# Heads of a linear attention in partition halves, zero rows written by count, and fewer weights split ahead

## The chip, the cores and the metric

The kernel runs on one core of a Trainium2 chip. The metric is the device time of one execution in microseconds (us). Engines: PE is TensorE (matmuls and transposes), DVE is VectorE, ACT is ScalarE, POOL is GpSimd, and SP issues most of the transfers.

## The reference, cut to what matters

Three stages on 3072 tokens (4 batches of 768), model width 384 (8 heads of 48).

```python
# 1: linear attention with a decaying state, per batch b and head h
for t in range(S):
    y[t]  = r[t] @ (state + outer(u * k[t], v[t]))
    state = w[:, None] * state + outer(k[t], v[t])
# 2: each token goes to one of 8 experts (384 -> 1024 -> 384, relu)
e_idx = argmax(x @ w_gate)
out[mask] = gate_w * sigmoid(x @ w_output_gate)[e] * (relu(x[mask] @ w1[e]) @ w2[e])
# 3: a dense layer pair, 384 -> 2048 -> 384
h = x @ w_in;  y = (h * cos(h)) @ w_out
```

## The kernel before, in words

The order of instructions on every engine is that of the program text; nothing is rescheduled.

**Attention** (`attention`). The 24 units are chunks of 128 tokens, unit i being chunk i // 4 of batch i % 4. With the decay powers `pw` and their inverses `ip`, a chunk becomes matrix products: `tr` transposes k (scaled to `kc` by POOL in `kprep`) and r, two heads (96 partitions) at a time. ACT copies the transposed k twice, each time with the mask `jm` that zeroes the other head, so that the score product of a head (L307, 96 rows) meets zeros in the rows of its neighbour. DVE scales the transposed r (L298) and masks the scores (L309). `state` multiplies r with the running state Z of the batch (L319, a 96x96 block per pair of heads; `blk` in `wd` keeps its off-diagonal blocks zero) and updates Z by L325, L327 and L328. `outp` adds scores times v (L341, output rows in two halves of 64) and DVE adds the bonus term (L343). Then `xt`, `logits` and, per batch of up to four units, `route1`, `prefix` and `route2` find the expert of each token and its row in the DRAM buffer `xd`, to which POOL scatters the token (L114). POOL also makes `rk` (L270, L273) and `dv` (L279), which waits for the row sums `dd` of DVE (L277).

In loop round i the text has: loads of unit i + 3, POOL's preparation of unit i + 2, `tr(i + 1)`, `scores(i)`, `xt(i - 1)`, `state(i)`, `logits(i - 1)`, routing, `dsum(i + 1)`, `outp(i)`, `prefix`. In rounds 1 to 4 SP writes zeros over the first 416 rows of each of the 8 regions of `xd`. In rounds 5 to 13 the first five pairs of expert weights are loaded, and from round 8 on they are split (`split_w`: ACT rounds to fp32r, DVE takes the remainder).

**Experts** (`moe`). After the attention come two branches that are not taken here (`any_decay` at L593, `overflow` at L695), which all engines pass. Then 64 steps, 8 blocks of 128 hidden columns for each expert. Step s loads and splits weights ahead (raw tiles in a ring of three, split tiles in a ring of seven), runs `l1` of its own block, `low` (DVE, the remainder of relu) of step s - 1 and `l2` of step s - 2. The rows of the next expert are loaded at block 0. **Dense layers** (`mlp2`) follow; they are not touched.

Of the kernel before, what the change touches and what calls it, by code (L numbers as in the profile page):

```python
# [28 lines left out]
NP = H // 2  # L29
NU = B * NCH  # L30
# [5 lines left out]
REG = N + OV  # L36
# [8 lines left out]
PRE = 5  # L45
# [18 lines left out]
class Program:  # L64
    def __init__(self, ctx, tc, r, k, v, w, u, w_gate, w_og, w1, w2, w_in, w_out, out):
# [10 lines left out]
        self.xd = dram.tile([E * REG, ROW], F32, name="xd")  # L76
        self.xg = dram.tile([S, B * DM], F32, name="xg")
# [119 lines left out]
    def attention(self, ctx):  # L197
# [9 lines left out]

        def load(i):
            c, b = divmod(i, B)
            for src, dst, nm in ((self.k, kt, "kt"), (self.r, rt, "rt"), (self.v, vt, "vt")):  # L210
                t = p2.tile([C, H, D], F32, tag=nm, name=nm, bufs=4 if nm == "vt" else 3)
# [3 lines left out]
        wT = ps.tile([96, NP], F32, tag="sm", name="wTp")  # L215
        nc.tensor.transpose(wT, self.wrow, ident[:NP, :NP])
# [9 lines left out]
        jm = cp.tile([96, 2], F32, name="jm")  # L226
        blk = cp.tile([96, 96], F32, name="blk")
        nc.gpsimd.memset(blk, 0.0)
        nc.gpsimd.affine_select(out=blk, in_=blk, compare_op=ALU.is_gt, fill=1.0, base=1 - D, pattern=[[-D, 2], [0, D]], channel_multiplier=1)
        nc.gpsimd.affine_select(out=blk, in_=blk, compare_op=ALU.is_ge, fill=0.0, base=0, pattern=[[-D, 2], [0, D]], channel_multiplier=1)  # L230
        nc.gpsimd.tensor_copy(jm, blk[:, ::D])

        pw = cp.tile([96, NP, C + 1], F32, name="pw")
        ip = cp.tile([96, NP, C], F32, name="ip")
# [3 lines left out]
        wTp, wT = wT, cp.tile([96, NP], F32, name="wT")  # L238
        nc.scalar.copy(wT, wTp)

        def double(t, o, n, eng):
            eng.tensor_tensor(t[:, :, o + n:o + 2 * n], t[:, :, o:o + n], t[:, :, o + n - 1:o + n].to_broadcast([96, NP, n]), ALU.mult)
# [18 lines left out]
        pwk = cp.tile([C, NP, 96], F32, name="pwk")  # L261
# [19 lines left out]
        def tr(i):  # L281
            s = st.setdefault(i, {})
            kT = ps.tile([96, NP, C], F32, tag="kT", name="kT")
            s["kT"] = p2.tile([96, NP, 2, C], F32, name="kTs")
            kk = s["kc"] if i else kt[i].rearrange("p (a j) d -> p a (j d)", j=2)
# [4 lines left out]
            rT = ps.tile([96, NP, C], F32, tag="rT", name="rT")  # L290
            rr = rt[i].rearrange("p (a j) d -> p a (j d)", j=2)
            for p in range(NP):
                nc.tensor.transpose(rT[:, p, :], rr[:, p, :], ident)
            s["rT"] = p2.tile([96, NP, C], F32, name="rTs")
            for p in ((slice(0, NP),) if i else (slice(0, 2), slice(2, 4))):
                if i == 0:
                    nc.vector.tensor_tensor(s["kT"][:, p], s["kT"][:, p], bc(ip[:, p], 2, 2), ALU.mult)
                nc.vector.tensor_tensor(s["rT"][:, p], rT[:, p], pw[:, p, 0:C], ALU.mult)  # L298

        def scores(i):  # L300
            s = st[i]
            s["A"] = []
            for q in range(2):
                A = ps.tile([C, 4, C], F32, tag=f"A{q}", name="A")
                for j in range(4):
                    h = 4 * q + j
                    nc.tensor.matmul(A[:, j, :], s["kT"][:, h // 2, h % 2, :], s["rT"][:, h // 2, :], start=True, stop=True)  # L307
                As = p2.tile([C, 4, C], F32, tag=f"As{q}", name="As")
                nc.vector.tensor_tensor(As, A, bc(amask, 1, 4), ALU.mult)  # L309
                s["A"].append(As)  # L310

        def state(i):
            s = st[i]
            c, b = divmod(i, B)
            if c:
                y = ps.tile([C, NP, 96], F32, tag="y", name="y")
                s["y"] = y
# [4 lines left out]
            P = ps.tile([96, NP, 96], F32, tag="P", name="P")  # L322
            vv = vt[i].rearrange("p (a j) d -> p a (j d)", j=2)
            for p in range(NP):
                nc.tensor.matmul(P[:, p, :], s["kc"][:, p, :], vv[:, p, :], start=True, stop=True)  # L325
            if c:
                nc.vector.tensor_tensor(Z[b], P, Z[b], ALU.add)  # L327
                nc.vector.tensor_tensor(Z[b], Z[b], wd, ALU.mult)  # L328
            else:
                Z[b] = cp.tile([96, NP, 96], F32, name=f"Z{b}")  # L330
                nc.vector.tensor_tensor(Z[b], P, wd, ALU.mult)

        def outp(i):
            s = st[i]
            c, b = divmod(i, B)
            y = s["y"] if c else ps.tile([C, NP, 96], F32, tag="y", name="y")
            for h in range(H):
                p, j = divmod(h, 2)
                for q in range(2):
                    t = slice(q * 64, q * 64 + 64)  # L340
                    nc.tensor.matmul(y[t, p, j * D:(j + 1) * D], s["A"][h // 4][:, h % 4, t], vt[i][:, h, :], start=(c == 0 and h == 0), stop=(h == H - 1))  # L341
            x = new_x(i)
            nc.vector.tensor_tensor(x[:, 0:DM], y.rearrange("p a d -> p (a d)"), s["dv"].rearrange("p h d -> p (h d)"), ALU.add)  # L343
# [16 lines left out]
        def logits(i):  # L360
# [3 lines left out]
            lg = ps.tile([128, 2 * E], F32, tag="sm", name="lg")  # L364
# [25 lines left out]
        def prefix(k):  # L390
            j, n = batches[k]
            for b in range(n):
                nc.vector.tensor_tensor(self.pf[:, j + b + 1, :], self.pf[:, j + b, :], self.ohall[:, j + b, :], ALU.add)

        def route2(k):
# [3 lines left out]
            rk = ps.tile([128, B, E], F32, tag="sm" if k < K - 1 else "xT", name="rkp")[:, 0:n]  # L399
# [39 lines left out]
        def totals():  # L439
            cnt = ps.tile([128, E], F32, tag="sm", name="cntp")  # L440
# [17 lines left out]
        def any_decay():  # L458
            st_ = p2.tile([96, 2, B * NP, D], F32, tag="kTs", name="gen_s")
            vs_ = p2.tile([96, 2, B * NP, D], F32, tag="As0", name="gen_v")  # L460
# [3 lines left out]
            uT = cp.tile([96, NP], F32, name="uT")  # L464
            nc.sync.dma_start(uT, self.u.rearrange("(p j) d -> (j d) p", j=2))
            nc.vector.memset(state_, 0.0)
# [40 lines left out]
        for p in range(NP):  # L507
            nc.tensor.transpose(tp[:, p * 96:(p + 1) * 96], ip[:, p, :], ident[:96, :96])
        nc.scalar.copy(pwk.rearrange("p a d -> p (a d)"), tp[:, :DM])
# [9 lines left out]
        wd = cp.tile([96, NP, 96], F32, name="wd")  # L519
# [350 lines left out]
```

## Time and profile before

| | us |
|---|---|
| median of 3 runs | 832.38 |
| lowest and highest | 830.17, 834.43 |
| the profiled execution, its own time | 830.15 |
| its span | 828.2 |
| PE busy in the span | 790.0 |
| DVE busy | 563.5 |
| ACT busy | 390.6 |
| POOL busy | 208.4 |

The attention fills the first 176 us or so, the experts run from about 186 to 410 us, the dense layers from there to the end. A matmul of f32 operands shows as two records. The idle time behind a group is that of its engine just before it, with what ended it.

### The profile page before, as it was taken

The numbers are of one execution on the slowest core, as the hardware profiler recorded it, in microseconds if no ns is written. First come the engines' busy times: TensorE is split into PE (matmuls) and PEld (weight loads), VectorE is DVE, ScalarE is ACT, GpSimd is POOL, SyncE is SP. The second block draws the span as 40 slices with busy tenths as digits, with TensorE's granted clock in tenths as the row PEclk, the third lists the DMA queues.
The fourth block names the chain that finished last, engine by engine and source line by source line (L and its number), as shares of the span: only waits on it lengthen the run. The fifth ranks groups of instructions, "written<-read, shape, count | busy, mean of one in ns | idle before, by whom it ended". The sixth has DMA issues, their size and how long they took to land.

```text
span 828.2 us, 14233 instructions
## 1 busy us (share of the span) xinstructions
PE 790.0 (95%) x5329; PEld 739.3 (89%) x5329; DVE 563.5 (68%) x987; ACT 390.6 (47%) x680; POOL 208.4 (25%) x290
## 2 busy tenths in 40 slices
PE   7989999929999999999999999999999999999996
PEld 7988899829999999999979999999999999988885
DVE  7778999736767777677376767767675555655653
ACT  3334343314555455545275655546464544445442
POOL 7667777620000000000021111111111122331332
PEclk9999999968999999999999999999999999999998
DMA  9897765136656654664201202102100201211211
GB/s 175 234 209 175 157 128 124 68 86 166 185 155 182 183 161 131 182 175 134 39 1 38 77 1 77 43 36 76 40 39 1 76 20 59 77 39 38 77 69 47
DMA packets 131304, 82.38 MB, mean 99 GB/s; under 512 B 83483, under 2 KB 123771, under 8 KB 131219
## 3 DMA queue, kind: packets, MB, share of 16 engines
q1 hardware_dynamic: 127717, 71.64, 32.5%
q0 software_dynamic: 3072, 9.45, 3.1%
q8 instruction: 45, 0.74, 0.4%
q14 instruction: 41, 0.33, 0.1%
q10 hardware_dynamic: 429, 0.21, 0.1%
HBM read 61.98 MB, written 19.31 MB: 98 GB/s over the span
## 4 chain that ended last, share of the span: by engine, by line
PE 72%; issue 2%; POOL 1%; DVE 1%; ACT 1%; POOLq 0%; ACTq 0%
PE h L756 8%; PE o L800 7%; PE h L757 7%; PE o L798 7%; PE o L799 7%; PE h L755 7%; PE h L627 4%; PE h L625 4%; PE acc L645 4%; PE h L626 4%; PE acc L647 4%; PE acc L646 4%; PE trp L608 1%; POOL out L114 1%; POOL nn L765 0%
## 5 line engine op out<-in xcount | busy, mean ns | idle before, releaser
L765 POOL TENSOR_SCALAR nn<-tt 128x512 f32<-128x512 f32 x96 | 60.1, 626 | 545.5 <-ACT tt L763 533.4
L766 DVE SCALAR_TENSOR_TENSOR tt<-nn,tt 128x512 f32<-128x512 f32 x96 | 66.4, 692 | 120.1 <-POOL nn L765 120.1
L763 ACT ACTIVATE tt<-h,quart 128x512 f32<-128x512 f32 x96 | 65.9, 686 | 77.4 <-PE h L757 76.9
L779 ACT CAST ga<-tt 128x512 fp32r<-128x512 f32 x96 | 59.7, 622 | 74.4 <-PE o L799 66.9
L159 DVE TENSOR_TENSOR wring<-raw,wring 128x768 fp32r<-128x768 f32 (+1 forms) x69 | 61.9, 897 | 45.9 <-ACT wring L158 45.9
L780 DVE TENSOR_TENSOR gc<-tt,ga 128x512 fp32r<-128x512 f32 x96 | 66.9, 697 | 17.7 <-ACT ga L779 17.6
L158 ACT CAST wring<-raw 128x768 fp32r<-128x768 f32 (+1 forms) x69 | 54.4, 788 | 44.1 <-PE acc L647 37.3
L800 PE MATMUL o<-wfix,gc 128*128 128x384 f32 x216 | 72.9, 338 | 0.1
L798 PE MATMUL o<-wfix,ga 128*128 128x384 f32 x216 | 72.7, 337 | 0.0
L799 PE MATMUL o<-wfix,ga 128*128 128x384 f32 x216 | 72.5, 336 | 0.0
L645 PE MATMUL acc<-hh,wring 128*128 128x416 f32 x192 | 69.0, 359 | 0.0
L771 ACT ACTIVATE tt<-tt 128x512 f32<-128x512 f32 x96 | 60.5, 630 | 17.7 <-DVE tt L766 17.7
L627 PE MATMUL h<-xs,wring 128*128 128x416 f32 x192 | 68.0, 354 | 0.0
L625 PE MATMUL h<-xs,wring 128*128 128x416 f32 x192 | 68.0, 354 | 0.0
L626 PE MATMUL h<-xs,wring 128*128 128x416 f32 x192 | 67.8, 353 | 0.0
L647 PE MATMUL acc<-hh,wring 128*128 128x416 f32 x192 | 67.1, 349 | 0.0
L646 PE MATMUL acc<-hl,wring 128*128 128x416 f32 x192 | 67.1, 349 | 0.0
L772 DVE TENSOR_TENSOR tt<-h,tt 128x512 f32<-128x512 f32 x96 | 65.7, 685 | 1.3 <-ACT tt L771 0.7
L756 PE MATMUL h<-ys,wfix 128*128 128x512 f32 x162 | 64.0, 395 | 0.2 <-DVE ys L747 0.2
L755 PE MATMUL h<-ys,wfix 128*128 128x512 f32 x162 | 63.1, 390 | 1.1 <-ACT ys L746 1.1
L757 PE MATMUL h<-ys,wfix 128*128 128x512 f32 x162 | 64.1, 395 | 0.0
L629 ACT ACTIVATE hh<-h 128x416 fp32r<-128x416 f32 x64 | 33.1, 517 | 52.8 <-PE h L627 49.9
(170 smaller groups left out, 1919.6 us busy)
## 6 DMA issues: line engine op xcount, KB each, us to landing
raw<-in_moe_w SPq DMA_DIRECT2D x128, 192.0 KB
raw<-in_moe_w_in SPq DMA_DIRECT2D x16, 384.0 KB
raw<-in_moe_w_out SPq DMA_DIRECT2D x16, 384.0 KB
xd<-rows SPq DMA_DIRECT2D x8, 625.6 KB
kt<-in_k SPq DMA_DIRECT2D x24, 192.0 KB
rt<-in_r SPq DMA_DIRECT2D x24, 192.0 KB
vt<-in_v SPq DMA_DIRECT2D x24, 192.0 KB
part<-osb SPq DMA_DIRECT2D x6, 768.0 KB
```

The costliest lines, as they stand in the source:

```text
L625: nc.tensor.matmul(h, wh, xh[:, kk, :], start=(kk == 0), stop=False)
L626: nc.tensor.matmul(h, wh, xl[:, kk, :], start=False, stop=False)
L627: nc.tensor.matmul(h, wl, xh[:, kk, :], start=False, stop=(kk == KD - 1))
L645: nc.tensor.matmul(acc[e][d], wh, a, start=(fb == 0), stop=False)
L646: nc.tensor.matmul(acc[e][d], wh, b, start=False, stop=False)
L647: nc.tensor.matmul(acc[e][d], wl, a, start=False, stop=(fb == NF1 - 1))
L755: nc.tensor.matmul(h, wh, xh[:, kk, :], start=(kk == 0), stop=False)
L756: nc.tensor.matmul(h, wh, xl[:, kk, :], start=False, stop=False)
L757: nc.tensor.matmul(h, wl, xh[:, kk, :], start=False, stop=(kk == KD - 1))
L798: nc.tensor.matmul(acc[k][q], a[:, sl], wh, start=(g == first), stop=False)
L799: nc.tensor.matmul(acc[k][q], a[:, sl], wl, start=False, stop=False)
L800: nc.tensor.matmul(acc[k][q], c[:, sl], wh, start=False, stop=(g == end))
```

## The change

Heads lie in halves of the partitions: each head has 64 rows, 48 used and 16 zero, so a pair of heads fills 128. The score and state products take 48 rows from partition 0 or 64, the state is 128x192 instead of 96x384, and the masked copies of k are gone; the k and r tiles are padded to 64 columns. The tile `y` takes two PSUM banks, and logits and ranks share the bank of `xT`. The copy of token ids goes to POOL, as do the prefix passes of all batches but the last three. Only region 0 of `xd` and a block of zeros in DRAM (`zd`) are written during the attention; for experts 1 to 7, `clear_rows` writes 416 zero rows behind the tokens of a region, from DRAM to DRAM, at an address from the count. Three weight pairs are loaded during the attention and none is split there: two are split after `totals`, and the expert loop catches up.

```diff
-REG = N + OV
+REG = N + CAP
-PRE = 5
+PRE = 2
+NRAW = 3
+        self.zd = dram.tile([CAP, ROW], F32, name="zd")
...
-        self.wrow = cp.tile([NP, 96], F32, name="wrow")
-        nc.sync.dma_start(self.wrow, self.w.rearrange("(p j) d -> p (j d)", j=2))
+        self.wrow = cp.tile([NP, 2, HP], F32, name="wrow")
+        nc.vector.memset(self.wrow, 1.0)
+        nc.sync.dma_start(self.wrow[:, :, 0:D], self.w.rearrange("(p j) d -> p j d", j=2))
...
+    def clear_rows(self, e):
+        c = self.nc.values_load(self.cnt_i[0:1, e:e + 1], engines=[ET.SP], min_val=0, max_val=N)
+        self.nc.sync.dma_start(self.xd[ds(c + e * REG, CAP)].rearrange("(p t) d -> p t d", t=4), self.zd.rearrange("(p t) d -> p t d", t=4))
...
+        wide = {nm: [cp.tile([C, H, HP], F32, name=f"{nm}{a}") for a in range(3)] for nm in ("kw", "rw")}
+        for a in range(3):
+            for nm in ("kw", "rw"):
+                (nc.vector if a == 0 else nc.gpsimd).memset(wide[nm][a][:, :, D:HP], 0.0)
+        k0 = cp.tile([C, H, HP], F32, name="k0")
+        nc.vector.memset(k0[:, :, D:HP], 0.0)
...
         def kprep(i, eng=nc.gpsimd):
-            kc = p2.tile([C, NP, 96], F32, name="kc", bufs=3)
-            eng.tensor_tensor(kc, kt[i].rearrange("p (a j) d -> p a (j d)", j=2), pwk, ALU.mult)
+            kc = wide["kw"][i % 3]
+            eng.tensor_tensor(kc[:, :, 0:D], kt[i], pwk, ALU.mult)
...
-            for j in range(2):
-                nc.scalar.activation(s["kT"][:, :, j, :], kT, AF.Copy, scale=jm[:, j:j + 1])
+            s["kT"] = p2.tile([128, NP, C], F32, name="kTs")
+            nc.scalar.copy(s["kT"], kT)
...
+        def rows_of(t, p, j):
+            return t[j * HP:j * HP + D, p, :]
...
-            for q in range(2):
-                A = ps.tile([C, 4, C], F32, tag=f"A{q}", name="A")
-                for j in range(4):
-                    h = 4 * q + j
-                    nc.tensor.matmul(A[:, j, :], s["kT"][:, h // 2, h % 2, :], s["rT"][:, h // 2, :], start=True, stop=True)
+            A = [ps.tile([C, NP, C], F32, tag=f"A{j}", name="A") for j in range(2)]
+            for p in range(NP):
+                for j in range(2):
+                    nc.tensor.matmul(A[j][:, p, :], rows_of(s["kT"], p, j), rows_of(s["rT"], p, j), start=True, stop=True)
...
+        def y_tile():
+            return ps.tile([C, 2, 512], F32, tag="y", name="y")[:, :, 0:NP * D].rearrange("t j (p e) -> t j p e", e=D)
...
-                    nc.tensor.matmul(y[:, p, :], s["rT"][:, p, :], Z[b][:, p, :], start=(p == 0), stop=False)
+                    for j in range(2):
+                        nc.tensor.matmul(y[:, j, p, :], rows_of(s["rT"], p, j), rows_of(Z[b], p, j), start=(p == 0), stop=False)
...
-                nc.tensor.matmul(P[:, p, :], s["kc"][:, p, :], vv[:, p, :], start=True, stop=True)
+                for j in range(2):
+                    nc.tensor.matmul(P[j * HP:(j + 1) * HP, p, :], s["kc"][:, 2 * p + j, :], vt[i][:, 2 * p + j, :], start=True, stop=True)
             if c:
-                nc.vector.tensor_tensor(Z[b], P, Z[b], ALU.add)
-                nc.vector.tensor_tensor(Z[b], Z[b], wd, ALU.mult)
+                nc.vector.tensor_tensor(P, P, Z[b], ALU.add)
...
+            nc.vector.tensor_tensor(Z[b], P, wd, ALU.mult)
...
-            nc.vector.tensor_copy(xs[i][:, DM:ROW].bitcast(I32), ids[:, c, b:b + 1])
+            nc.gpsimd.tensor_copy(xs[i][:, DM:ROW].bitcast(I32), ids[:, c, b:b + 1])
...
-            lg = ps.tile([128, 2 * E], F32, tag="sm", name="lg")
+            lg = ps.tile([128, 2 * E], F32, tag="xT", name="lg")
...
-                nc.vector.tensor_tensor(self.pf[:, j + b + 1, :], self.pf[:, j + b, :], self.ohall[:, j + b, :], ALU.add)
+                (nc.vector if k >= K - 3 else nc.gpsimd).tensor_tensor(self.pf[:, j + b + 1, :], self.pf[:, j + b, :], self.ohall[:, j + b, :], ALU.add)
...
-            if 1 <= i <= E // 2:
-                for e in (2 * i - 2, 2 * i - 1):
-                    nc.sync.dma_start(self.block(e * REG), zero)
-            if i >= 5 and i % 2 == 1 and (i - 5) // 2 < PRE:
-                self.load_w((i - 5) // 2)
+            if i in (2, 3):
+                nc.sync.dma_start(self.block(0) if i == 2 else self.zd.rearrange("(p t) d -> p t d", t=4), zero)
+            if i in (12, 15, 18):
+                self.load_w(i // 3 - 4)
...
-            if i >= 8 and pre:
-                self.split_w(*pre.pop(0))
...
         totals()
+        for j in range(PRE):
+            self.split_w(j)
...
-        nconv, made, nload = 7 * NFIX, 0, PRE
+        nconv, made, nload, nsplit = 7 * NFIX, 0, NRAW, PRE
         for s, (e, fb) in enumerate(steps):
-            while nload <= min(s + LEAD + 2, len(steps) - 1):
+            while nload < min(nsplit + NRAW, len(steps)):
                 self.load_w(nload)
                 nload += 1
-            if PRE <= s + LEAD < len(steps):
-                self.split_w(s + LEAD)
+            while nsplit <= min(s + LEAD, 2 * s + 3, nload - 1):
+                self.split_w(nsplit)
+                nsplit += 1
...
-                if e + 1 < E:
-                    self.load_rows(e + 1)
+                if e == 0:
+                    self.clear_rows(1)
+            if e + 1 < E and fb == (0 if e else 2):
+                self.load_rows(e + 1)
+            if e + 2 < E and fb == 4:
+                self.clear_rows(e + 2)
```

## Rows read from the trace of the kernel before

**Rows 1.** Windows: stretch, length, busy us of engines with counts, PE clock, transfers.

```profile
110.00:130.00 20.00, 18.74 (x261) 17.86 (x260) 18.73 (x41) 7.43 (x19) 14.62 (x15) 1.00 0.56 116
...
150.00:160.00 10.00, 8.77 (x94) 8.19 (x92) 7.94 (x20) 4.11 (x9) 6.39 (x8) 0.83 0.11 38
```

**Rows 2.** Timeline of PE, one unit: start, length, line, tiles, records.

```profile
110.55 0.55 PE L356 MATMUL xT<-ident,x 128*128 128x128 f32 x3
110.94 1.03 PE L319 MATMUL y<-Z,rTs 96*128 96x96 f32 x8
111.80 0.84 PE L325 MATMUL P<-vt,kc 128*96 128x96 f32 x8
112.58 0.53 PE L368 MATMUL lg<-wgo,xTs 128*64 128x16 f32 x12
112.95 1.12 PE L341 MATMUL y<-vt,As 128*64 128x48 f32 x32
114.00 0.64 PE L287 MATMUL kT<-ident,kc 128*96 128x128 f32 x4
...
114.91 1.95 PE L307 MATMUL A<-rTs,kTs 96*128 96x128 f32 x16
116.72 0.55 PE L356 MATMUL xT<-ident,x 128*128 128x128 f32 x3
```

**Rows 3.** Timeline of PE: the same step in units 4 and 21.

```profile
34.19 0.49 PE L356 MATMUL xT<-ident,x 128*128 128x128 f32 x3
...
149.50 0.55 PE L356 MATMUL xT<-ident,x 128*128 128x128 f32 x3
```

**Rows 4.** Groups of DVE by line and form, 0 to 182 us.

```profile
L309 DVE TENSOR_TENSOR As<-A,amask 128x512 f32<-128x512 f32 x48 | 31.3, 681 | 3.0 <-PE A L307 2.8 <-issue 0.2
...
L328 DVE TENSOR_TENSOR Z<-Z,wd 96x384 f32<-96x384 f32 x16 | 21.3, 1333 | 0.6
...
L393 DVE TENSOR_TENSOR pf<-pf,ohall 128x8 f32<-128x8 f32 x24 | 11.3, 471 | 0.6
...
L327 DVE TENSOR_TENSOR Z<-P,Z 96x384 f32<-96x384 f32 x16 | 8.8, 552 | 7.5 <-PE P L325 7.5
```

**Rows 5.** Timeline of POOL, one unit.

```profile
104.46 1.00 POOL L265 TENSOR_TENSOR kc<-kt,pwk 128x384 f32<-128x384 f32 x1
105.42 0.99 POOL L270 TENSOR_TENSOR rk<-rt,kt 128x384 f32<-128x384 f32 x1
106.57 1.01 POOL L114 DMA_INDIRECT xd<-x,slot  x1 [0.16 <-issue]
107.60 1.01 POOL L273 TENSOR_TENSOR rk<-rk,u_bc 128x384 f32<-128x384 f32 x1
109.58 1.08 POOL L279 TENSOR_TENSOR dv<-vt,dd 128x384 f32<-128x384 f32 x1 [0.96 <-DVE dd L277]
```

**Rows 6.** Waits, 30 to 150 us: us in total, times, longest.

```profile
POOL kc L265 <- DMA kt<-in_k: 6.4, 2, 3.5
```

**Rows 7.** Small passes of POOL and ACT by line and form, 0 to 182 us.

```profile
L372 ACT COPY L<-lg 128x16 f32<-128x16 f32 x23 | 3.9, 171 | 30.5 <-PE lg L368 27.2 <-PE y L341 1.8 <-PE P L325 1.5
...
L242 POOL TENSOR_TENSOR pw<-pw 96x64 f32<-96x64 f32 x1 | 0.3, 291 | 0.6 <-DVE pw L242 0.6
...
L231 POOL COPY jm<-blk 96x2 f32<-96x2 f32 x1 | 0.2, 182 | 0.1
```

**Rows 8.** Line 593, the first branch: DVE's record.

```profile
L593 DVEq COMPARE_BRANCH  x1: 72/72/72, 176.3 to 176.3; - x1
```

**Rows 9.** Timeline, 189 to 199 us: the expert stage begins.

```profile
189.96 0.39 SPq L138 DMA_DIRECT2D raw<-in_moe_w  x1
...
194.70 0.35 PE L645 MATMUL acc<-hh,wring 128*128 128x416 f32 x1
...
197.22 0.84 ACT L158 CAST wring<-raw 128x768 fp32r<-128x768 f32 x1 [1.00 <-DMA raw<-in_moe_w]
...
198.09 0.96 DVE L159 TENSOR_TENSOR wring<-raw,wring 128x768 fp32r<-128x768 f32 x1 [1.23 <-ACT wring L158]
```

More of the change, by code (lines that the diff above doesn't have):

```diff
@@ L29 @@
 NP = H // 2
+HP = 64
 NU = B * NCH
@@ L210, in load @@
             for src, dst, nm in ((self.k, kt, "kt"), (self.r, rt, "rt"), (self.v, vt, "vt")):
-                t = p2.tile([C, H, D], F32, tag=nm, name=nm, bufs=4 if nm == "vt" else 3)
+                if nm == "rt":
+                    t = wide["rw"][i % 3][:, :, 0:D]
+                elif nm == "kt" and i == 0:
+                    t = k0[:, :, 0:D]
+                else:
+                    t = p2.tile([C, H, D], F32, tag=nm, name=nm, bufs=4 if nm == "vt" else 3)
                 nc.sync.dma_start(t, src[b, :, c * C:(c + 1) * C, :].rearrange("h p d -> p h d"))
                 dst[i] = t
-        wT = ps.tile([96, NP], F32, tag="sm", name="wTp")
-        nc.tensor.transpose(wT, self.wrow, ident[:NP, :NP])
+        wT = ps.tile([128, NP], F32, tag="xT", name="wTp")
+        nc.tensor.transpose(wT, self.wrow.rearrange("p j d -> p (j d)"), ident[:NP, :NP])
         load(0)
@@ L225, in attention @@
         make_upper_triangular(nc, amask, 1.0, diag=False)
[L226 to L234, printed above, removed]
+        pw = cp.tile([128, NP, C + 1], F32, name="pw")
+        ip = cp.tile([128, NP, C], F32, name="ip")
         wc = pw[:, :, 1]
@@ L295, in tr @@
[L295 to L298, printed above, removed]
+            s["rT"] = p2.tile([128, NP, C], F32, name="rTs")
+            if i == 0:
+                nc.vector.tensor_tensor(s["kT"], s["kT"], ip, ALU.mult)
+            nc.vector.tensor_tensor(s["rT"], rT, pw[:, :, 0:C], ALU.mult)
@@ L335, in outp @@
             c, b = divmod(i, B)
-            y = s["y"] if c else ps.tile([C, NP, 96], F32, tag="y", name="y")
+            y = s["y"] if c else y_tile()
             for h in range(H):
@@ L340, in outp @@
                     t = slice(q * 64, q * 64 + 64)
-                    nc.tensor.matmul(y[t, p, j * D:(j + 1) * D], s["A"][h // 4][:, h % 4, t], vt[i][:, h, :], start=(c == 0 and h == 0), stop=(h == H - 1))
+                    nc.tensor.matmul(y[t, j, p, :], s["A"][j][:, p, t], vt[i][:, h, :], start=(c == 0 and p == 0), stop=(p == NP - 1))
             x = new_x(i)
-            nc.vector.tensor_tensor(x[:, 0:DM], y.rearrange("p a d -> p (a d)"), s["dv"].rearrange("p h d -> p (h d)"), ALU.add)
+            cols = lambda t: t.rearrange("t (p j e) -> t j p e", j=2, e=D)
+            nc.vector.tensor_tensor(cols(x[:, 0:DM]), y, cols(s["dv"].rearrange("t h e -> t (h e)")), ALU.add)
             vt.pop(i)
@@ L398, in route2 @@
             oh = self.ohall[:, j:j + n, :]
-            rk = ps.tile([128, B, E], F32, tag="sm" if k < K - 1 else "xT", name="rkp")[:, 0:n]
+            rk = ps.tile([128, B, E], F32, tag="xT" if k < K - 1 else "P", name="rkp")[:, 0:n]
             rf = rk.rearrange("p b e -> p (b e)")
@@ L439, in totals @@
         def totals():
[L440 removed]
+            cnt = ps.tile([128, E], F32, tag="P", name="cntp")
             nc.tensor.matmul(cnt, ones, self.pf[:, NU, :], start=True, stop=True)
@@ L463, in any_decay @@
             yo = p2.tile([2, B * NP * D], F32, tag="As1", name="gen_y")
-            uT = cp.tile([96, NP], F32, name="uT")
+            uT, wT = (cp.tile([96, NP], F32, name=nm) for nm in ("uT", "wgen"))
             nc.sync.dma_start(uT, self.u.rearrange("(p j) d -> (j d) p", j=2))
+            nc.sync.dma_start(wT, self.w.rearrange("(p j) d -> (j d) p", j=2))
+            jm = cp.tile([96, 2], F32, name="jm")
+            nc.gpsimd.memset(jm, 0.0)
+            nc.gpsimd.affine_select(out=jm, in_=jm, compare_op=ALU.is_gt, fill=1.0, base=1 - D, pattern=[[-D, 2]], channel_multiplier=1)
+            nc.gpsimd.affine_select(out=jm, in_=jm, compare_op=ALU.is_ge, fill=0.0, base=0, pattern=[[-D, 2]], channel_multiplier=1)
             nc.vector.memset(state_, 0.0)
@@ L507, in attention @@
         for p in range(NP):
-            nc.tensor.transpose(tp[:, p * 96:(p + 1) * 96], ip[:, p, :], ident[:96, :96])
-        nc.scalar.copy(pwk.rearrange("p a d -> p (a d)"), tp[:, :DM])
+            nc.tensor.transpose(tp[:, p * 128:(p + 1) * 128], ip[:, p, :], ident)
+        nc.scalar.copy(pwk, tp.rearrange("p (h d) -> p h d", d=HP)[:, :, 0:D])
         kprep(0, nc.vector)
@@ L518, in attention @@
         nc.vector.tensor_scalar(self.pf[:, 0, :], ebase, 1.0 / 128, None, ALU.mult)
-        wd = cp.tile([96, NP, 96], F32, name="wd")
-        nc.vector.tensor_tensor(wd, pw[:, :, C:C + 1].to_broadcast([96, NP, 96]), bc(blk, 1, NP), ALU.mult)
-        ne = cp.tile([96, NP], F32, name="ne")
+        wd = cp.tile([128, NP, D], F32, name="wd")
+        nc.vector.tensor_copy(wd, pw[:, :, C:C + 1].to_broadcast([128, NP, D]))
+        ne = cp.tile([128, NP], F32, name="ne")
         nc.vector.tensor_tensor(ne, wc, wT, ALU.not_equal)
-        pre = [(j, part) for j in range(PRE) for part in range(2)]
         for i in range(NU):
@@ L572, in attention @@
             if i == 1:
-                fa = ps.tile([128, NP], F32, tag="sm", name="fa")
-                nc.tensor.matmul(fa, ones[:96, :], ne, start=True, stop=True)
+                fa = ps.tile([128, NP], F32, tag="xT", name="fa")
+                nc.tensor.matmul(fa, ones, ne, start=True, stop=True)
                 faf = cp.tile([128, 1], F32, name="faf")
```

34 lines of the change are left out of this document (15 added, 19 removed).

## The prediction, made before the result

> **What bounds the kernel now.** I read the windows first, stage by stage. After about 186 us the tensor engine is busy almost all the time in code the diff barely touches, so the change must earn its time in the attention, before that, and may lose some where the experts begin. In the attention two engines are near their limit at once: in the stretch 110 to 130 us PE is busy 18.74 us of 20 and DVE 18.73; ACT has room (7.43) [rows 1]. The timeline of PE gives the loop. A unit (one chunk of 128 tokens of one batch) that waits for nothing lasts 6.17 us, 110.55 to 116.72, and its steps follow from the starts: transposes of x 0.39, y from the state 0.86, P 0.78, router logits 0.37, output 1.05, transposes of k and r 0.91, scores 1.81 [rows 2]. From unit 4 to unit 21, which start at 34.19 and 149.50, there are 17 periods, so the mean is 6.78 us [rows 3]: 0.61 us over the undisturbed unit goes to routing matmuls and to waits.
>
> DVE explains those waits. The two state passes have the same 96x384 shape, but the one that reads PSUM takes 552 ns and the one with both inputs in SBUF 1333; the prefix, 8 columns wide, takes 471 [rows 4]. Passes with both inputs in SBUF are held up beside POOL. POOL works 5.1 us a unit and waits 0.96 for DVE [rows 5]. Early on, POOL also waited 6.4 us for k tiles while SP's queue carried the zero blocks [rows 6].
>
> **PE's part of the change.** Scores: still 16 records, now on 48 rows in alternating partition halves. Today a record takes 1.81/16 = 0.113 us. No row shows two row halves at work, so the price lies between 0.113 (in turn) and 0.057 (fully side by side). The nearest row is the output step, whose column halves alternate in the same order: 32 records in 1.05, 0.033 each, whereas P with 96 columns takes 0.78/8 = 0.097; 64 columns in turn would take about 0.065, so halves do run side by side there [rows 2]. I take 0.058: 0.93 instead of 1.81. The Trainium skill (TensorE: Matmul & The Clock Gate, Measured speedup vs the span model) gives 3.07x for four row tiles, which leans the same way; no row here shows it.
>
> y from the state doubles to 16 records, each with 128 columns of weights and only 48 moving. The present 8 take 0.108 each, hardly under the 0.113 of 128 columns, so weights set the pace: 16 x 0.058 = 0.93 side by side, 1.73 in turn, against 0.86. P becomes 16 records shaped like the output step: 16 x 0.033 = 0.53 instead of 0.78. The transposes have the scores' width, 8 x 0.113 = 0.90, unchanged.
>
> The unit now passes between full, row-half and column-half shapes five times instead of twice. The Trainium skill (TensorEngine Tiling (Array Packing), Key Properties) says that changing the mode drains the engine. The rows show two changes per unit already: the 8 transposes after the output step take 0.91, 0.114 each, no more than the scores without a change [rows 2]. By the rows three more cost at most some 0.2; if each emptied the pipe for the 0.14 by which the scores' busy time (1.95) exceeds their spacing (1.81), 0.42, and the forecast would be some 4 us worse over 20 units. I take 0.2. PE's unit: 0.39 + 0.93 + 0.53 + 0.37 + 1.05 + 0.91 + 0.93 + 0.2 = 5.3 us.
>
> **DVE and POOL.** DVE today spends 18.73/20 x 6.78 = 6.35 us a unit. It loses the two state passes and the prefix, 1.33 + 0.55 + 0.47, and gains two passes of 192 columns that both read PSUM. 512 columns take 0.681 and 384 take 0.552, 1 ns a column, so 0.36 each. That leaves 4.7 [rows 1, 4]. The split weight passes go too. DVE stops being a bound.
>
> POOL keeps 1.00 + 0.99 + 1.01 + 1.01 + 1.08 and 0.16 of issue, 5.25 [rows 5], and gets the id copy and, for most batches, one prefix pass a unit. A 96x2 copy took 182 ns on it and a 96x64 product 291 [rows 7]; between 0 and those, I take 0.35: 5.6 us, just above PE. With 0.15 for routing units and jitter the period is 5.75.
>
> ACT copies k once instead of twice; with ACT at 7.43 of 20 that is worth nothing by itself. Sharing one PSUM bank between xT, logits and ranks costs nothing: those steps already follow each other through ACT's copies; uncovered it would be a wait per unit of one copy of the logits, 0.17 [rows 7].
>
> **The sum.** Units 4 to 20: 17 x (6.78 - 5.75) = -17.5. Units 0 to 3 have no state product: scores save 0.88 each, -3.5, and the zero traffic (eight blocks before, two now) no longer delays k. Units 21 to 23: scores -2.6, and the low clock in 150 to 160 us (0.83, so 3.4 us at 1.2 GHz, 1.7 lost) should go with the long prefix on DVE: -4 in all. Attention: -25.
>
> Against that, splits 0 and 1 now stand behind the totals on DVE. DVE reaches the first branch at 176.3 [rows 8] and the others meet it behind that; ACT's casts fit its idle time, DVE's two passes of 0.96 [rows 9] don't: +1.9. Taking this for hidden behind the landing rows would be 0.
>
> Then the experts start with two split weights instead of five. In the first steps loads 3 and 4, the clear of expert 1 (626 KB), and load 5 stand in SP's queue in this order; before, loads 5 and 6, the rows of expert 1 and load 7 did. That load 7 was issued at 189.96 and held ACT until 197.22 [rows 9]. Load 5 in the same place would be split at 197.22 + 0.84 + 0.96 = 199.0. Behind split 5 on DVE stands the remainder of step 0 (0.6 by the slope above), and the second layer, which started at 194.70 [rows 9], waits for it: 4.9 us of stall, between 0 (the load lands early) and 7. After such a gap I count one low-clock stretch, 1.7 as above [rows 1]. The clears of experts 2 to 7 go four steps ahead of their use, beside an expert stage with spare transfer time; +1 for loads they delay, 0 to 4. Against: 1.9 + 4.9 + 1.7 + 1 = 9.5.
>
> Net -15.5. The profiled execution took 830.15, so 814.7; it lies 2.2 below the median of the three runs. I say **816 us**.
>
> **Rivals.**
> The halves of rows run in turn (10%). Scores stay 1.81 and the state product becomes 1.73: PE 7.0, period 7.2, 17 x 0.45 = +8; little is saved elsewhere (-2), and the 9.5 stay: some **847 us**. It decides from a record price of 0.078 us, where 32 records in 23 units eat the net gain (15.5/23/32 = 0.021 over 0.058). For it: no row shows row halves. Against it: the column halves of the output step.
>
> POOL becomes the bound with its present wait (14%). If it still waits 0.96 for DVE in each unit, the period is 5.6 + 0.96 = 6.5: -5 instead of -17.5, net -3, **829**, about no change. Against: the pass DVE waits behind, 1333 ns, is the one that shrinks.
>
> No stall at the experts (12%): load 5 lands before it is wanted, only 1.9 + 1 remain, **808**; with a period of 5.5, 803.
>
> The clock falls more often (6%). At 150 to 160 us it fell though PE was busy 8.77 us of 10 [rows 1]. With more small gaps, such a fall in each fourth unit costs 6 x 1.7 = 10: **826**.
>
> **Chances and range.** The forecast (58%) spans 809 to 822, by a period of 5.5 to 6.0 and a stall of 0 to 7. A measurement of this kernel can tell about 0.5% (828.2 to 836.5) from no change. Faster: the forecast, the missing stall, and the better parts of the POOL and clock cases, 0.81. Same: the rest of those two, 0.09. Slower: the halves in turn, 0.10. The range 803 to 829 leaves out that last case and little else.
>
> **What would show it.** In the changed trace: 16 score records within about 1 us, and 16 state records in no more; unit starts 5.6 to 5.9 us apart; the state passes on DVE at 0.36; POOL with almost no idle time; a gap on PE of some 5 us before the second layer's first records of expert 0, waiting for DVE behind the split of weight 5. I am wrong if score records stay 0.11 apart, if POOL still waits for dd in each unit, or if waits for weights appear in the later experts.

## The result and the profile after

The changed kernel takes 823.48 us (median of four runs, 821.0 to 827.77), the kernel before in the same session 832.5 (830.17 to 834.43). The ratio is 0.9898, with a 95% interval of 0.9849 to 0.9948: faster, by 9.0 us, where 16.4 from the median were forecast. The profiled execution took 822.72 us (span 821.0); the one before took 830.15 (span 828.2). The spans differ by 7.2 us, and the two traces place all of it. Ratios, here and below, leave out executions more than 1.5% above the quickest of the same kernel; medians count all.

Windows of the changed kernel, with the columns of [rows 1]:

```profile
110.00:130.00 20.00, 19.41 (x366) 17.33 (x363) 14.14 (x32) 5.72 (x14) 18.48 (x23) 1.00 0.66 172
130.00:150.00 20.00, 19.51 (x207) 17.12 (x204) 12.62 (x37) 6.12 (x16) 12.14 (x23) 0.61 0.15 55
150.00:160.00 10.00, 7.87 (x80) 7.01 (x79) 4.40 (x27) 2.98 (x9) 3.04 (x6) 0.50 0.11 40
180.00:190.00 10.00, 6.84 (x31) 6.36 (x30) 5.95 (x10) 4.87 (x7) 0.00 (x0) 0.88 0.67 197
```

DVE's 18.73 us of 20 [rows 1] have become 14.14: it is no bound any more, PE is. But the granted clock at the end of the attention is now 0.61 and then 0.50; 0.50 is the lower of PE's two levels, 1.2 GHz.

PE's timeline of the changed kernel, to be laid beside [rows 2, 3]: the start of unit 4, one undisturbed unit, and the place where the clock falls.

```profile
32.38 0.55 PE L373 MATMUL xT<-ident,x 128*128 128x128 f32 x3
...
68.21 0.55 PE L373 MATMUL xT<-ident,x 128*128 128x128 f32 x3
68.69 1.10 PE L336 MATMUL y<-Z,rTs 48*128 48x48 f32 x16
69.72 0.67 PE L342 MATMUL P<-vt,kw 128*64 128x48 f32 x16
70.22 0.49 PE L385 MATMUL lg<-wgo,xTs 128*64 128x16 f32 x12
70.55 1.12 PE L357 MATMUL y<-vt,As 128*64 128x48 f32 x32
71.60 0.66 PE L299 MATMUL kT<-ident,kw 128*128 128x128 f32 x4
72.09 0.60 PE L305 MATMUL rT<-ident,rw 128*128 128x128 f32 x4
72.62 1.16 PE L319 MATMUL A<-rTs,kTs 48*128 48x128 f32 x16
73.72 0.55 PE L373 MATMUL xT<-ident,x 128*128 128x128 f32 x3
...
132.00 0.52 PE L373 MATMUL xT<-ident,x 128*128 128x128 f32 x3
132.44 1.09 PE L336 MATMUL y<-Z,rTs 48*128 48x48 f32 x16
133.47 0.53 PE L385 MATMUL lg<-wgo,xTs 128*64 128x16 f32 x12
134.36 0.43 PE L418 MATMUL rkp<-pf,ones 128*128 128x32 f32 x2 [0.36 <-POOL kw L278]
134.60 0.61 PE L419 MATMUL rkp<-ohall,amask 128*128 128x32 f32 x2
135.15 1.95 PE L357 MATMUL y<-vt,As 128*64 128x48 f32 x32
```

A unit lasts 5.51 us, 68.21 to 73.72, instead of 6.17. Scores take 1.10 (72.62 to 73.72), the state product 1.03, P 0.50. From unit 4 to unit 21 there are 99.62 us, 5.86 a unit instead of 6.78. Then, at the rank matmuls of unit 21, behind a wait of 0.36, the output step grows from 1.12 to 1.95 us with its 32 records unchanged: PE has fallen to 1.2 GHz.

The kernel before falls in its unit 21 too, behind waits at the same place:

```profile
151.90 0.38 PE L401 MATMUL rkp<-pf,ones 128*128 128x32 f32 x2 [0.53 <-DVE pf L393]
152.11 0.39 PE L402 MATMUL rkp<-ohall,amask 128*128 128x32 f32 x2
153.20 1.64 PE L341 MATMUL y<-vt,As 128*64 128x48 f32 x32 [0.70 <-DVE As L309]
```

Unit 21 took 9.18 us there (149.50 to 158.68) and takes 8.94 here. The difference lies behind it: units 22 and 23 took 5.23 and 3.54 at a granted clock of 1.00 (158.68 to 167.45) and take 7.24 and 6.91 at 0.50 (140.94 to 155.09). The clock does not come back before 182 us.

Where the 7.2 us came from, each step being the change of the distance between two records that both traces have:

| from, to | before | after | difference | forecast |
|---|---|---|---|---|
| start to unit 4 | 34.19 | 32.38 | -1.8 | -3.5 |
| unit 4 to 21 | 115.31 | 99.62 | -15.7 | -17.5 |
| unit 21 to the last scatter's issue | 23.89 | 30.28 | +6.4 | -4 |
| to the first expert's transposes | 12.47 | 10.50 | -2.0 | (splits) +1.9 |
| expert stage | 229.66 | 235.58 | +5.9 | +6.6 and +1 |
| dense layers to the end | | | 0 | 0 |

The expert stage begins with the stall that was forecast. Timeline of the changed kernel, all engines, to be laid beside [rows 9]:

```profile
184.02 0.35 PE L665 MATMUL acc<-hh,wring 128*128 128x416 f32 x1
185.15 0.83 ACT L166 CAST wring<-raw 128x768 fp32r<-128x768 f32 x1 [2.88 <-DMA raw<-in_moe_w]
186.02 0.96 DVE L167 TENSOR_TENSOR wring<-raw,wring 128x768 fp32r<-128x768 f32 x1 [2.75 <-ACT wring L166]
...
186.90 0.58 DVE L655 SCALAR_TENSOR_TENSOR hl<-h,hh 128x416 fp32r<-128x416 f32 x1
187.53 0.46 PE L666 MATMUL acc<-hl,wring 128*128 128x416 f32 x1 [3.16 <-DVE hl L655]
```

Read it upwards from PE: the second layer waits for the remainder `hl`, which stands on DVE behind a weight's split, which waits for ACT's cast, which waits for the weight to land. It costs 3.16 us. Most of the rest of the +5.9 lies ahead of it: from the transposes to the first record of the second layer 11.24 us (172.78 to 184.02) instead of 8.84 (185.86 to 194.70), with a wait of 0.74 and a clock of 0.57 instead of 0.68 over that stretch.

This +2.4 and the -2.0 in the line above it belong together. From the last scatter's issue to the first record of the second layer it took 21.31 us before (173.39 to 194.70) and takes 21.74 now (162.28 to 184.02). In the twelve traces below it takes 19.0 to 22.4, with weights split early or late, so neither figure by itself can be put down to the change.

Groups of DVE and POOL of the changed kernel by line and form, 0 to 170 us, beside [rows 4, 7]:

```profile
L347 DVE TENSOR_TENSOR Z<-P,wd 128x192 f32<-128x192 f32 x20 | 7.1, 356 | 0.9 <-PE P L342 0.3
L344 DVE TENSOR_TENSOR P<-P,Z 128x192 f32<-128x192 f32 x16 | 5.9, 367 | 14.4 <-PE lg L385 7.2 <-PE P L342 6.4 <-issue 0.8
L367 POOL COPY x<-ids 128x1 int32<-128x1 int32 x24 | 4.4, 184 | 0.0
L410 POOL TENSOR_TENSOR pf<-pf,ohall 128x8 f32<-128x8 f32 x20 | 4.0, 199 | 1.2
```

### The profile page after: what moved, and what is told of

It reads as the page before. It is cut to its first block, busy times and chain, and to the rows that moved or that the text cites. A ratio compares the mean times of both kernels' runs of the same rounds, so it can differ in the third digit from the quotient of the medians.

```text
span 821.0 us, 14842 instructions
## 1 busy us (share of the span) xinstructions
PE 784.1 (95%) x5649; PEld 723.1 (88%) x5649; DVE 534.0 (65%) x940; ACT 375.6 (46%) x651; POOL 211.9 (26%) x334
## 4 chain that ended last, share of the span: by engine, by line
PE 72%; issue 2%; POOL 1%; DVE 1%; ACT 1%; DMA 1%; SPq 0%; POOLq 0%; DVEq 0%; ACTq 0%
PE h L781 8%; PE o L825 7%; PE h L782 7%; PE o L823 7%; PE o L824 7%; PE h L780 7%; PE acc L665 4%; PE acc L666 4%; PE acc L667 4%; PE h L647 4%; PE h L646 4%; PE h L645 4%; PE trp L628 1%; POOL out L118 1%; DMA raw<-in_moe_w 1%
## 5 line engine op out<-in xcount | busy, mean ns | idle before, releaser
L167 DVE TENSOR_TENSOR wring<-raw,wring 128x768 fp32r<-128x768 f32 x64 | 61.2, 957 | 47.9 <-ACT wring L166 47.9
L166 ACT CAST wring<-raw 128x768 fp32r<-128x768 f32 x64 | 53.4, 836 | 49.8 <-PE acc L667 36.4
L823 PE MATMUL o<-wring,ga 128*128 128x384 f32 x168 | 57.2, 340 | 0.0
```

The costliest lines, as they stand in the source:

```text
L823: nc.tensor.matmul(acc[k][q], a[:, sl], wh, start=(g == first), stop=False)
```

## The experiments

The theory: the halves run side by side because they alternate, and what the change failed to give was lost to PE's clock at the end of the attention. Its rivals: halves cost what they cost in any order; DVE's relief alone does the work, without halves; the late splits, not the clock, cost the missing time. Ratios are to the kernel before on the same chip; intervals are 95%.

**In turn.** Order of the loops in the scores, and likewise in the state product (the heads of the loops alone are shown):

```
-for p in range(NP):
-    for j in range(2):
+for j in range(2):
+    for p in range(NP):
```

> The changed kernel, but the scores and the product with the state go through all four pairs for the lower partition half first and then for the upper, so that records of different halves no longer alternate. Theory: the halves of rows run side by side only where they alternate; then a score record takes about 0.11 us instead of 0.068 and a state record about 0.108 instead of 0.064, a unit 1.4 us longer, 23 units: +25 to +30, about 850. Rival: the time of a record comes from the 48 rows or from the reordering of weight loads, not from alternation; unchanged at 823.

Measured: 1.0546 [1.0505, 1.0587], 880.98 us, runs from 871.77 to 888.29. PE's timeline, a unit at the full clock, from an execution of 885.29 us:

```profile
131.99 0.55 PE L373 MATMUL xT<-ident,x 128*128 128x128 f32 x3
132.47 1.58 PE L336 MATMUL y<-Z,rTs 48*128 48x48 f32 x16
...
136.88 1.71 PE L319 MATMUL A<-rTs,kTs 48*128 48x128 f32 x16
138.52 0.55 PE L373 MATMUL xT<-ident,x 128*128 128x128 f32 x3
```

Same records, other order: scores 1.64 instead of 1.10, state 1.50 instead of 1.03, the unit 6.53 instead of 5.51. The rival about the order falls: the same records are slower in turn. But two things alternate in the changed kernel, the row half and the PSUM bank that is written (`A[0]` and `A[1]`, the two banks of `y`), and this edit takes both away; no run tells them apart. The output step alternates column halves inside one bank at 0.033 a record, so halves of columns need no change of bank. The ratio lies 0.065 above the changed kernel's, some 54 us. The records make 1.0 us a unit, some 24 us, of that; for most of the rest there is the clock, 0.68 over 30 to 130 us of this trace with PE busy 98.89 of 100, and 0.93 on average in the two quickest executions, where the changed kernel had 0.965 to 0.974. Units at the low clock last over 10 us (41.25 to 52.47, 52.47 to 62.86). Why this order lowers the clock, no run tells.

**P kept.** The early return of the last chunk's units stands behind the P records instead of ahead of them, so units 20 to 23 compute a P that nobody reads.

> The changed kernel, but the four units of the last chunk (20 to 23) also run the 16 records of the state product P, whose result nobody reads. Theory A: the attention's gain shrinks at its end because PE falls to 1.2 GHz in unit 21 (134.5 us) and stays there until 182 us, and the four units without P are what lets it fall; with P the clock stays high through unit 23 and the last scatter comes about 5 us earlier, total about 818. Rival B: the end of the attention is a chain of small passes on DVE, ACT and POOL that the clock of PE hardly touches; P only adds 4 x 0.5 us (1.0 each at the low clock), total 824 to 827. If A holds but these records are too little to hold the clock, the clock row stays at 0.5 to 0.6 and the total is as under B; the run with full-array records tells that apart.

Measured: 0.9877 [0.9847, 0.9908], 819.7 us, not to be told from the changed kernel. In its trace (an execution of 829.86 us, above the other three at 816.95 to 821.49) the clock is still 0.74 over 130 to 150 us and 0.50 from 150 to 180. In this execution keeping P did not hold the clock; the other three, with a mean clock of 0.973 to 0.979 against the changed kernel's 0.965 to 0.974, have no trace.

**Filler.** In units 20 to 23, eight full-array records (`ident` times `ones`) go to P's bank in P's place.

```
 if c == NCH - 1:
+    F = ps.tile([128, 4, C], F32, tag="P", name="fill")
+    for p in range(4):
+        nc.tensor.matmul(F[:, p, :], ident, ones, start=True, stop=True)
     return
```

> The changed kernel, with 8 extra records in each of units 20 to 23 that use all 128 rows and columns (identity times ones, read by nobody). Theory A: these keep PE at 2.4 GHz through unit 23; units 21 and 22 last about 6.3 us (5.4 and 0.86 of filler) instead of 8.9 and 7.2, and the last scatter comes 3 to 5 us earlier, total 818 to 820. Rival B: the clock is immaterial at the end, so the filler adds 4 x 0.86 us, total 825 to 827.

Measured: 0.9916 [0.9885, 0.9947], 822.06 us, where 818 to 820 were expected. Windows:

```profile
30.00:130.00 100.00, 98.39 (x1664) 88.04 (x1662) 71.08 (x164) 28.88 (x70) 78.65 (x111) 0.91 0.63 141
130.00:150.00 20.00, 19.64 (x303) 17.41 (x300) 12.64 (x34) 7.10 (x18) 15.59 (x24) 1.00 0.33 106
```

The clock stayed at 1.00 to 150 us, behind the wait of 0.36 in unit 21 as well, and unit 21's start to the totals' matmul took 23.8 us (138.35 to 162.15) instead of 29.7 (132.00 to 161.73), though some 3 us of filler were added. But in 30 to 130 us, where nothing was edited, the clock fell to 0.91. So the price of the low tail is shown, some 6 us and the filler on top; a gain in the whole is not.

**Changed again.** The changed kernel once more, in another session.

> The changed kernel itself, run once more beside the others. Theory A2: the clock falls to 1.2 GHz at the rank matmuls of a unit that computes ranks (units 5, 9, 13, 17, 21), not in each of them and not in the same ones in each execution, and each fall costs about 7 us (two units of 9 us instead of 5.5). Then this execution's unit starts show 1 to 3 long pairs, each beginning at such a unit, and the times scatter over some 6 us around 0.99 of before. Rival: the fall belongs to the last chunk alone (unit 21 on), and is in the same place again.

Measured: 0.9902 [0.9864, 0.994], 823.44 us, with runs from 819.76 to 836.45. In its trace the clock falls at unit 17 (108.72 to 116.78, 8.06 us) and again at unit 21. The place of the falls differs between executions of one program; the one at unit 21 came in both, and behind the same wait of 0.36.

**Rank late.** For the first five batches `route2` moves behind the output step.

> The changed kernel, with the rank matmuls and passes of the first five batches put behind the output step of their unit, where PE doesn't wait 0.36 us for ACT's copy of the logits. Theory A2 with the wait as what lets the clock fall: no falls before unit 22, units 21 and 22 at 5.5 us each, total 4 to 7 us under the changed kernel (0.982 to 0.985 of before). Rival: the fall follows from the small records of these units whatever their place; then the falls stay, about as many, and the total is within 2 us of the changed kernel.

Measured: 1.0084 [1.0056, 1.0112], 836.87 us: a miss. PE's timeline:

```profile
69.48 0.90 PE L373 MATMUL xT<-ident,x 128*128 128x128 f32 x3 [2.56 <-DVE tdr L428]
70.31 1.95 PE L336 MATMUL y<-Z,rTs 48*128 48x48 f32 x16
```

The ranks share xT's PSUM bank, so the next transposes now wait until DVE has read the ranks (its pass `tdr`), and the unit behind that wait runs at the low clock, 9.79 us (69.48 to 79.27). In unit 21 itself, where the wait of 0.36 is gone too and no such wait follows, the theory held: 5.67 us (145.65 to 151.32) at a clock of 1.00.

**Combined.** Rank late, early splits (below) and filler together.

> The changed kernel with three edits at once: weights split during the attention as before, ranks behind the output step, and 8 full-array records in each of units 20 to 23. Theory: no low clock until the end of unit 23 and no stall at the experts; the early splits give 3 to 4 us, the held clock 5 to 7 less 3.4 of filler: 8 us under the changed kernel, 0.978 to 0.982 of before. Rival: the falls move elsewhere in the attention; then no better than the early splits alone, 0.985.

Measured: 1.0014 [0.9983, 1.0045], 835.21 us, runs from 827.32 to 847.99: a miss. The waits of rank late for `tdr` are in its trace, up to 2.9 us, so it says little of the two other edits.

**Rank bank.** The text stays; the ranks of the first five batches get the bank of `kT` instead of that of `xT`.

```
-rk = ps.tile([128, B, E], F32, tag="xT" if k < K - 1 else "P", name="rkp")[:, 0:n]
+rk = ps.tile([128, B, E], F32, tag="kT" if k < K - 3 else "xT" if k < K - 1 else "P", name="rkp")[:, 0:n]
```

> The changed kernel, with the ranks of the first five batches in the PSUM bank of the transposed k instead of that of xT and the logits, so that the rank matmuls no longer wait 0.36 us for ACT's copy of the logits. Theory A3: the small wait in these units is what lets the clock fall; then units 5 to 21 show no fall, the long pairs of 9 us are gone, 5 to 7 us less than the changed kernel, 0.982 to 0.985, with less scatter. Rival: falls come at these units without that wait too (the rank matmuls are short), the number of falls stays; 0.990.

Measured: 0.9863 [0.9841, 0.9885], 816.85 us, runs from 816.28 to 819.13. PE's timeline from unit 21 on:

```profile
132.45 0.55 PE L373 MATMUL xT<-ident,x 128*128 128x128 f32 x3
...
134.41 0.41 PE L418 MATMUL rkp<-pf,ones 128*128 128x32 f32 x2
134.65 0.39 PE L419 MATMUL rkp<-ohall,amask 128*128 128x32 f32 x2
134.97 1.14 PE L357 MATMUL y<-vt,As 128*64 128x48 f32 x32
...
138.15 0.55 PE L373 MATMUL xT<-ident,x 128*128 128x128 f32 x3
...
153.89 0.56 PE L458 MATMUL cntp<-pf,ones 128*128 128x8 f32 x2 [1.34 <-DVE pf L410]
```

Without the wait of 0.36 the output step stays at 1.14, unit 21 lasts 5.70 us instead of 8.94, and the totals' matmul comes 21.4 us after unit 21's start instead of 29.7. The clock is 1.00 over 30 to 130 us as well. The routing units pay for it: 7.44 us (61.07 to 68.51, a wait of 1.2 for DVE's `tdr` in it) instead of 6.74 (61.47 to 68.21). That wait, three times as long as the one removed, was followed by no fall here, in none of units 9, 13 and 17. In the trace of three edits (below), which has the same banks, it was followed by one:

```profile
65.68 0.86 PE L299 MATMUL kT<-ident,kw 128*128 128x128 f32 x4 [1.23 <-DVE tdr L431]
66.34 1.06 PE L305 MATMUL rT<-ident,rw 128*128 128x128 f32 x4
67.33 2.08 PE L319 MATMUL A<-rTs,kTs 48*128 48x128 f32 x16
```

So the length of a wait does not decide by itself, and the new bank does not keep the clock up everywhere. At unit 21 the runs agree: the clock fell in all five traces with alternating halves that have the wait of 0.36 there and no filler (the changed kernel's two, P kept, early splits, split lag), and stayed at 1.00 in the two where only the ranks' bank or place was changed (rank bank, rank late) and in the three with filler in that unit (filler, combined, three edits). The stall at the experts stays, 3.1. The ratio lies between what the theory (0.982 to 0.985) and its rival (0.990) gave, and its interval just overlaps those of the changed kernel's two measurements, so the gain in the whole is likely, not shown.

**Early splits.** Five weight pairs loaded and split in the attention as before, none behind the totals; all else as changed.

> The changed kernel, but with the five weight pairs loaded and split during the attention as before (rounds 5 to 13 and from round 8 on), none after the totals. Theory: the expert stage then starts without the stall of 3.2 us in front of the second-layer records and without the 0.7 us wait ahead of the first block; the attention's period stays at 5.86 us because DVE has room (14 to 15 us busy of 20); total 3 to 4 us less, about 819.5. Rival: DVE's added 0.55 us in ten units and ACT's 0.5 delay the units by as much, total 823, unchanged.

Measured: 0.985 [0.9831, 0.9869], 816.98 us. The expert stage takes 231.3 us instead of 235.6 and has no wait at the second layer, and the attention does not pay for the splits as it did before: most of DVE's splits take 0.55, two 1.5. Combined, which splits early too, has no such wait and a stage of 230.8. So the late splits are a part of the missing time.

**Split lag.** The ramp of splits in the experts is made slower, so that an early step splits fewer weights ahead of its own remainder:

```
-while nsplit <= min(s + LEAD, 2 * s + 3, nload - 1):
+while nsplit <= min(s + LEAD, s + 3 + s // 8, nload - 1):
```

> The changed kernel, with another limit on the splits of the expert loop: one a step from step 1 on (s + 3 + s // 8 instead of 2 s + 3), so that split 5, whose load is late, no longer stands ahead of the remainder of step 0 on DVE. Theory: the second layer's 3.2 us wait for DVE in expert 0 goes and the second layer starts right behind the third first-layer block; nothing else changes; 3 us less than the changed kernel, 0.986 of before, within what falls of the clock scatter. Rival: another wait takes its place one step later (a weight not yet split), same time.

Measured: 0.981 [0.9787, 0.9833], 813.27 us, the fastest, level with three edits below; 0.986 was expected. Its timeline at the first second-layer block:

```profile
179.16 0.58 DVE L655 SCALAR_TENSOR_TENSOR hl<-h,hh 128x416 fp32r<-128x416 f32 x1
179.60 0.35 PE L665 MATMUL acc<-hh,wring 128*128 128x416 f32 x1
179.80 0.46 PE L666 MATMUL acc<-hl,wring 128*128 128x416 f32 x1
```

The remainder is in time. But the expert stage as a whole is 234.6 us, only 1.0 shorter; the second layer waits 1.5 for DVE's remainder later on. The two traces' spans differ by 5.9 us, and the other 4.9 lie ahead of the experts, where the code is the same: the clock fell at three routing units, yet at unit 21 it came back within the unit (7.63 us), and units 22 and 23 took 4.36 and 4.82. Why, no run tells. So the edit's own gain is some 1 us of it, by this trace; the rest is not shown to be its doing.

**DVE relief.** The kernel before with only the small edits: both state passes read PSUM, prefix and id copy on POOL; 96-row heads, five early splits.

> The kernel before, with only three edits: the first state pass writes PSUM and the second reads it, the prefix passes of the first batches and the id copies go to POOL. Heads stay in 96 rows, splits and zero blocks stay. Theory: DVE's passes with both inputs in SBUF made the waits of PE, so the period falls from 6.78 to about 6.3 us, the PE-bound unit of 6.17 plus routing: 17 x 0.45 = 8 us, 0.990 of before; the rest of the change's gain (6.3 to 5.86) is the halves'. Rival: without the smaller unit on PE nothing is gained, 6.7 to 6.8 us, 1.000.

Measured: 0.9991 [0.9968, 1.0014], 830.16 us: a miss, since a gain was expected. Timeline around one split:

```profile
80.70 1.01 POOL L273 TENSOR_TENSOR rk<-rk,u_bc 128x384 f32<-128x384 f32 x1
80.95 3.99 DVE L159 TENSOR_TENSOR wring<-raw,wring 128x384 fp32r<-128x384 f32 x1
81.66 0.83 POOL L279 TENSOR_TENSOR dv<-vt,dd 128x384 f32<-128x384 f32 x1
...
84.68 1.14 POOL L114 DMA_INDIRECT xd<-x,slot  x1 [0.16 <-issue]
84.86 0.55 DVE L343 TENSOR_TENSOR x<-y,dv 128x384 f32<-128x384 f32 x1
85.46 0.55 PE L356 MATMUL xT<-ident,x 128*128 128x128 f32 x3 [1.87 <-DVE x L343]
```

DVE's split has both inputs in SBUF. This one of the ten takes 3.99 us, where the median is 0.55, and ends just after POOL's first gap (0.16, ahead of 84.68); PE waits 1.87 for what stands behind it, and its next unit lasts 9.26 us (85.46 to 94.72) at a clock of 0.63.

**Relief, no splits.** The same, with the weights handled as in the change; heads in 96 rows, zero rows written early.

> The kernel before, with state passes through PSUM and prefix and id copies on POOL as in the relief run, and with the weights handled as in the change (three pairs loaded, none split in the attention). Heads stay in 96 rows, zero blocks as before. Theory: in the relief run the split passes, two inputs in SBUF, waited up to 3.99 us for a gap in POOL's work and PE waited behind them; without them the unit falls to 6.17 plus routing, about 6.35 (-7), and the stall at the experts costs 4 of it; 0.993 to 0.997 of before. The further step to 5.86 then belongs to the halves. Rival: the relief run was slow for its low clock alone; period 7, total 1.000 to 1.005.

Measured: 1.0031 [1.0013, 1.0049], 830.75 us: a miss, since 0.993 to 0.997 was expected. Its ordinary unit lasts 6.09 us (56.60 to 62.69), the mean of 13 units 6.34 (56.60 to 138.99), and at the experts it waits 5.1. So the small edits and the missing splits shorten the mean unit from 6.78 [rows 3] to 6.56 over the same 17, some 4 us, and the stall takes it back; by themselves they give nothing. An ordinary unit falls from 6.09 to 5.51 with the halves, and the steps that shrink are the scores and P: that is where the gain is, and the rival of relief alone falls.

**Three edits.** Split lag, rank bank and filler together.

> The changed kernel with the later splits, the ranks in the other bank and 8 full-array records in each of units 20 to 23. Theory: no stall at the experts (-3), the clock held until unit 23 (-6 net of the filler) and fewer falls before: 0.978 to 0.982 of before, the fastest of all. Rival: falls come anywhere in the attention and take back what the held end gives; 0.986.

Measured: 0.9813 [0.9792, 0.9835], 814.01 us. One fall of the clock between 30 and 150 us, the one in unit 9 shown under rank bank, an expert stage of 230.6, and still no more than split lag alone. The gains don't add.

Not tried: the zero rows alone written early again, and the small passes alone back on DVE.

## Why the prediction was right, and where not

**Halves side by side: right.** A score record cost 0.069 (1.10/16), a state record 0.064, between the bounds 0.057 and 0.113; 0.058 was taken. Run in turn, the same records cost 0.103 and 0.094. P (0.50 for 0.53) was right; the unit is 5.5, not 5.3. The Trainium skill (TensorEngine Tiling (Array Packing), Key Properties) says that a change of tiling mode drains the engine; the trace leaves little for it: the transposes ahead of the scores (kT and rT) take 1.02 instead of 0.91 [rows 2] and those behind them (x) 0.48 instead of 0.39, together the 0.2 that was taken.

**The period: right, by another engine.** 5.86 for 5.75, in part by luck. DVE lost its long passes as forecast: 356 and 367 ns for 0.36. But POOL was costed at 5.6, above PE; it needs 5.05 without a prefix pass (its `dv` starts at 96.45 and 101.50) and about 5.25 with one, since the id copy and prefix took 184 and 199 ns and each `dv` 0.84 instead of 1.08. PE sets the unit, with 5.5, and routing units and jitter, put at 0.15, take 0.35.

**Start: too much.** -1.8 for -3.5. A unit there went from 5.22 us (23.73 to 28.95) to 4.65 (23.03 to 27.68): the scores save some 0.7, not 0.88, and the transposes take back 0.2.

**The failed term: "the low clock in 150 to 160 us (0.83 ...) should go with the long prefix on DVE: -4 in all".** It did not go; it grew to 134.5 to 182 us, and the term came out at +6.4, 10 us off. The prediction tied the fall to DVE's long prefix, for which the ranks of unit 21 had waited 0.53. That prefix is gone (the four passes left to DVE take 202 ns each, where the mean was 471), and the fall stayed: it begins at the same rank matmuls, now behind a wait of 0.36 for ACT, which still reads the logits in the bank that the ranks are to write. (The row of unit 21 names POOL's `kw`, which ended last; that it is the bank shows in rank bank, where another bank takes the wait away.) The clock held there where only the ranks' bank or place was changed (rank bank, rank late) or where full-array records were added (filler). In rank bank, with the clock held to some 146 us, the totals' matmul comes 21.4 us after unit 21's start, where the kernel before took 23.8 (149.50 to 173.34): -2.4 of the forecast -4. The clock rival, given 6%, had the mechanism, and the trace has it in the tail alone; it priced a fall at 1.7 us, and one unit in it costs 1.3 (8.06 for a routing unit's 6.74) to 4.3 (9.79 for 5.51), more in the tail, where the clock did not come back.

**Late splits.** The splits behind the totals were costed at 1.9 with 0 as the other end; 0 it was. DVE's two passes end at 166.3 (164.45, and 1.83 for both), and the loads of the expert's rows are issued at 166.85, 4.57 us behind the last scatter; early splits, which has no pass there, has the same 4.58, and 10.39 to the transposes where the changed kernel has 10.50. That step was 12.47 before, and 10.2 to 13.1 in the twelve other traces, so the fall by 2.0 need not be the change's. The stall came at the place and by the chain that were forecast, 3.2 for 4.9; with early splits it is gone and the stage 4.3 shorter. The low clock behind it (1.7) did not come; ahead of it the way to the second layer grew by 2.4, which goes with the 2.0.

**Clears.** +1 with 0 as the other end. From the first record of the second layer to the dense layers the stage grew by 3.5, of which the stall is 3.16: under 0.4 is left.

By the table the terms on the bad side (tail 10.4, start 1.7, period 1.8) and those on the good side (branches 3.9, experts 1.7) leave 8.3: -7.2 instead of -15.5. That the time stayed inside the range owes something to errors on both sides. Why the clock falls at one routing unit and not at the next with the same wait, why it does not come back in the tail, and why split lag's attention was quicker, stays open.

## What to carry to other kernels

Let row halves alternate product by product (here each half had a PSUM bank of its own, too): in turn they were hardly quicker than full rows (0.103 for 0.113 a score record). When PE becomes the bound, read its clock stage by stage, and look for small PE waits in tight loops: a side computation that writes a bank which another engine is still reading makes one. Another bank removed it at unit 21 and put a longer one into the other routing units (rank bank, 0.9863, a likely gain). Then try how early weights are split: early splits took the stall away and made the stage 4.3 us shorter, the slower ramp left a wait of 1.5. Price an edit that shortens one engine by the engine that waits behind it: DVE's relief alone was worth nothing.

## What the runs showed of the hardware

In the changed kernel PE was busy 19.41 us of 20 at a granted clock of 1.00 (110 to 130 us); at 134.5 us, right behind a wait of 0.36, it fell from 2.4 to 1.2 GHz. With the halves in turn the granted clock was 0.68 over 100 us though PE was busy 98.89. A program's falls come in different units in different executions (21 alone; 17 and 21). Each fall shown here begins behind a wait of PE (0.36, 1.23, 1.87 and 2.56 us, and 0.53 and 0.70 in the kernel before), but not each such wait is followed by one.

A DVE pass with two SBUF inputs took 3.99 us instead of 0.55 beside a POOL that worked without a gap. The Trainium skill (SBUF — State Buffer, Who interferes with whom) says that such a pass and a POOL instruction that reads SBUF exclude each other; the trace agrees in kind, and shows the wait to last over several POOL instructions, from 80.95 to some 84.4 us (3.99 less 0.55), not one.
